# A matrix-memory recurrence and two feed-forward layers on one core: the first expert's weights fetched in 13 pieces of columns

## The chip, the core and the metric

The kernel runs on one core of one Trainium2 chip. The metric is the time of one execution in device microseconds (us), lower is better. The engines are TensorE (PE, its weight loads PEld), VectorE (DVE), ScalarE (ACT), GpSimd (POOL) and the queue of SyncE (SP), which here only issues DMAs. POOL issues the indirect DMAs, those whose rows are picked by an index in memory.

## The reference

The inputs are six arrays of 4 x 8 heads, 768 steps and 40 columns for the recurrence, and the weights of a mixture of 8 experts and of a dense layer. All arithmetic is float32.

```python
state = 0                                        # per head, 40 x 40
for t in range(768):
    y[:, :, t] = einsum('bhd,bhde->bhe', rt, state)
    Sa = einsum('bhde,bhe->bhd', state, at)
    state = state * wt - Sa (x) bt + vt (x) kt   # (x): outer product
x = y as 3072 tokens of 320
logits = x @ w_gate + modality_bias[modality_id]
e_idx = argmax(logits); gate = softmax(logits)[e_idx]
for e in range(8):                               # w1: 320 x 1024, w2: 1024 x 320
    out[mask] = gate * (relu(x[mask] @ w1[e]) @ w2[e])
h = out @ w_in                                   # 320 x 2048
return (h * sigmoid(1.702 * h)) @ w_out          # 2048 x 320
```

## The kernel before, in words

**Three stages.** The recurrence goes in 24 steps of 32 time steps (`NCH`), each turned into matmuls of small blocks; each step ends with a tile Y of 128 tokens x 320 columns. Then come the experts (`moe1`), which take the tokens sorted by expert in tiles of 128 rows, and the dense layer (`moe2`).

**Inside a step c of the recurrence.** `chain(c, g)` works for two groups g of four heads. It makes W from the state (W, X, V, all in PSUM), ends with the tile `ust`, and SP issues a DMA transpose of it, `UE<-ust`. `state` makes the next state (`S`, `s`, `Ss`, and the transpose `Sd<-s`). `output` multiplies `rE` and `UE` in 32 small matmuls (`g<-rE,UE`), masks the result (`mx`, `mgZ`, `zbd`) and multiplies it with `bst` into `y`; DVE makes Y of it. The last step, 23, needs the state of step 22, and its own `UE`.

**Routing.** `row` scales each Y, makes halves of it in `XR` and multiplies them with the gate's weights. Every fourth step, `route` picks the expert of each token of a group, and POOL scatters the rows of `XR` into a sorted table `XD` in memory with one indirect DMA for each step (`XD<-XR,desti`). The groups are steps 0-3, 4-7, 8-11, 12-15, 16-19, 20-22 and 23. One `XR` buffer serves all groups, so that the next group's `XR` waits until the scatters before it have landed. When all is routed, `tables` works out the order of the tiles, and `usual` decides a branch; behind it `moe1` begins.

**The first expert's weights.** After step 19 (`EARLY` is 20) `lead` picks the expert with the most tokens so far. Its number is in `er`, and `w0row` is the row of the weight tables for each partition. Two indirect DMAs bring the weights: `fetch(1)` 128 rows of 3072 numbers into `raw1`, `fetch(2)` 128 rows of 2560 numbers into `raw2`. Two more (`load`, `xg<-XD,xrow`) bring the first two tiles of that expert's rows. ACT and DVE cut the weights into two float16 halves (`split<-raw`), 8 parts of 384 columns and 5 of 512, and PE runs the first two tiles (`first`) between the last steps of the recurrence: the turn of the rows is `v<-id,xg`, the matmuls are `w<-aE,split` and `s<-split,...`.

**What sets the order.** Everything from the recurrence to `first` is recorded and then ordered by a planner (`Plan.emit`): a list scheduler with a cost for each operation, that goes forward and backward nine times (`ROUNDS`) and keeps the order with the shortest planned span. So an instruction's place on its engine follows from the planner's costs, not from the place in the code. For an indirect DMA it counts 1040 ns on POOL, a start of 2450 ns (`DMA_START`) and 0.355 ns for each byte of a partition, during which its one modelled DMA channel takes no other transfer. Between two indirect DMAs in a row POOL gets a `memset` of `between`. All recorded instructions have line 234.

Of the kernel before, what the change touches and what calls it, by code (L numbers as in the profile page):

```python
# [469 lines left out]
I32 = mybir.dt.int32  # L470
U32 = mybir.dt.uint32
AF = mybir.ActivationFunctionType
ALU = mybir.AluOpType
# [15 lines left out]
WS = 256.0  # L489
GROUPS = [(0, 4), (4, 4), (8, 4), (12, 4), (16, 4), (20, 3), (23, 1)]  # L490
EARLY = 20
FIRST = 2


class Mlp:
# [11 lines left out]
    def consts_in(self, p, tp, w_gate, modality, bias):  # L507
        nc = self.nc
# [15 lines left out]
        def iota(shape, pattern, base=0, mult=0):  # L524

            count[0] += 1
            t = tp.tile([128] + shape, I32, name=f"io{count[0]}")
            nc.gpsimd.iota(t, pattern=pattern, base=base, channel_multiplier=mult)
            f = p.tile([128] + shape, F32, name=f"if{count[0]}")
            nc.vector.tensor_copy(f, t)  # L530
            return f
# [6 lines left out]
        nc.vector.tensor_scalar(self.e3072, e4, float(NT), None, op0=ALU.mult)  # L538
        self.q = iota([NTILE], [[128, NTILE]], mult=1)
        self.pf = iota([1], [[0, 1]], mult=1)  # L540
        self.s1 = iota([NSLOT], [[1, NSLOT]], base=1)
        self.s128 = iota([NSLOT], [[128, NSLOT]], mult=1)

# [11 lines left out]
        m = tp.tile([128, NTILE], mybir.dt.int64, name="mod")  # L555
# [117 lines left out]
    def lead(self, ncol, ps):  # L673
# [20 lines left out]
        nc.vector.tensor_scalar(self.w0row, self.er[:, 0, 0:1], 128.0, self.pf, op0=ALU.mult, op1=ALU.add)  # L694
        nc.vector.tensor_scalar(self.xrow[:, 0:FIRST], self.s128[:, 0:FIRST], self.er[:, 1, 0:1], None, op0=ALU.add)

    def small(self, name, shape, dt=F32):
        if name not in self.tabs:
            self.tabs[name] = self.tab.tile([128] + shape, dt, name=name)
        return self.tabs[name]  # L700
# [105 lines left out]
    def weights1(self, wp, W1, W2):  # L806

        self.W1, self.W2 = W1, W2
        parts = []
        for n, w in ((1, NW1), (2, NW2)):  # L810
            raw = wp.tile([128, max(w, 2644)], F32, name=f"raw{n}")
            setattr(self, f"raw{n}", raw[:, 0:w])
            parts.append(raw)
        for n, w in ((1, NW1), (2, NW2)):
            t = wp.tile([128, w], F32, name=f"split{n}")
            h = t.bitcast(F16)
            setattr(self, f"hi{n}", h[:, 0:w])
            setattr(self, f"lo{n}", h[:, w:2 * w])
            parts.append(t)

        xg = wp.tile([128, 1032], F32, name="xg0")
        self.x0 = [xg[:, a:a + XROW] for a in (XROW, 0)]
        self.y0 = [xg[:, a:a + YROW] for a in (2 * XROW, XROW)]
        parts.append(xg)
        left = [[t, 0] for t in parts]

        def lend(n):
            x = next(x for x in left if x[1] + n <= x[0].shape[1])
            x[1] += n
            return x[0][:, x[1] - n:x[1]]  # L830

        return lend

    def fetch(self, n, row):
        self.nc.gpsimd.indirect_dma_start(
# [1003 lines left out]
def body(tc, A, out):  # L1839
    nc = tc.nc  # L1840
    with ExitStack() as ctx:
        m = Mlp(tc, ctx)
        dp = ctx.enter_context(tc.tile_pool(name="dr", bufs=1, space=DRAM))
        XD = m.XD = dp.tile([NE * NT, XROW], I32, name="XD")
        YS = m.YS = dp.tile([NSLOT * 128, YROW], I32, name="YS")
        XF = dp.tile([NT, DM], F32, name="XF")
        m.consts(A["wg"], A["mod"], A["mb"])
        kp = m.tab = ctx.enter_context(tc.tile_pool(name="keep", bufs=1))
        tail = NTILE - 1
        with ExitStack() as c1:  # L1850
            pool = lambda n, b: c1.enter_context(tc.tile_pool(name=n, bufs=b, side="right", reuse_waits="tile"))
            lent = m.weights1(pool("m1w", 1), A["W1"], A["W2"])
            with ExitStack() as c2:
                p = Pool(c2.enter_context(tc.tile_pool(name="rt", bufs=1)), 1)
                ps = Pool(c2.enter_context(tc.tile_pool(name="rps", bufs=1, space=PSUM)), 1)
                at = Attn(tc, c2, A["WU"], A["AB"], A["KVR"], kp, lent)
                plan = m.nc = at.plan
                plan.between = m.between
                Y, sent, read, later = {}, [], [], []

                def sink(c, full=False):
                    if not full:
                        Y[0] = p.tile([128, DM], F32, tag="Y", bufs=2)
                        return Y[0][:, :]
                    plan.after = RTAIL if c == tail else 0.0
                    plan.tail = TAIL if c >= EARLY else 0.0
                    m.row(Y[0][:, :], c, (p, lambda: ps.tile([128, 512], F32, tag="r")))
                    c0 = max(a for a, _ in GROUPS if a <= c)
                    if c == c0 + dict(GROUPS)[c0] - 1:
                        m.route(c0, XD, p, sent if c < EARLY else later)  # L1870
                    plan.tail = WTAIL
                    if c == EARLY - 1:
                        m.lead(EARLY, m.bank[:, 416:424])
                        for n in (1, 2):
                            m.fetch(n, m.w0row)
                        for i, x in enumerate(m.x0):
                            read.append(m.load(i, x))
                            plan.preds[read[-1]].update(sent)
                    plan.tail = TAIL if c == tail - 1 else 0.0

                at.run(sink)
                plan.tail, plan.after = 0.0, RTAIL
                m.tables(m.bank[:, 416:424])
                at.range(kp, m.ones, at.py.bank([8], "y"))
                ok, usual, usualf = m.small("ok", [1], I32), m.small("usual", [1], I32), m.small("usualf", [1])
                at.good(plan, ok, usualf, m)
                plan.vector.tensor_copy(usual, usualf)
                plan.tail, plan.after = LTAIL, 0.0
                for n in (1, 2):
                    m.split(n)  # L1890
                p1, p2 = at.spare()
                m.first(p1, Given(ys=m.y0), p2)
                plan.emit()
                sent, read, later = ([plan.made[i] for i in x] for x in (sent, read, later))
                apart(tc, sent + later)

                for a in read:
                    for b in later:
                        tc.declare_no_dep(a.ins, b.ins, reason="rows of later tiles")
                m.nc = nc  # L1900
            m.before2(ctx)
            m.tab = ctx.enter_context(tc.tile_pool(name="tab", bufs=1, reuse_waits="tile"))
            m.next(pool("m1x", 5))
            for i, x in m.x1.items():
                m.load(i, x)
            rv = nc.values_load(usual[0:1, 0:1], min_val=0, max_val=1)
            with tc.If(rv < 1):
                held = nc.values_load(ok[0:1, 0:1], min_val=0, max_val=1)
                with tc.If(held < 1):
                    slow_attention(tc, A["r"], A["k"], A["v"], A["w"], A["a"], A["b"], XF)  # L1910
                    with tc.tile_pool(name="rt3", bufs=1) as p, tc.tile_pool(name="rps3", bufs=1, space=PSUM) as ps:
                        for c in range(NTILE):
                            X = p.tile([128, DM], F32, tag="Y", name="Y")
                            nc.sync.dma_start(out=X, in_=XF[c * 128:(c + 1) * 128, :])
                            m.row(X, c, (p, lambda: ps.tile([128, 512], F32, tag="r", name="r")))
                            c0 = max(a for a, _ in GROUPS if a <= c)
                            if c == c0 + dict(GROUPS)[c0] - 1:
                                m.route(c0, XD, p)
                        m.lead(NTILE, ps.tile([128, NE], F32, tag="c", name="c"))
                        m.tables(ps.tile([128, NE], F32, tag="c", name="c"))  # L1920
                        for n in (1, 2):
                            m.fetch(n, m.w0row)
                            m.split(n)
                        for i, x in [*enumerate(m.x0), *m.x1.items()]:
                            m.load(i, x)
                        m.first(p, p, ps)
                with tc.tile_pool(name="rt4", bufs=1) as p, tc.tile_pool(name="rps4", bufs=1, space=PSUM) as ps:
                    m.extra(p, ps)
            step = m.weights2(A["wi"], A["wo"], ctx)
            m.moe1(lambda i: step())  # L1930
        m.moe2(out)
# [16 lines left out]
```

## Time and profile before

| | us |
|---|---|
| median of 3 runs | 1115.99 |
| the three runs | 1117.01, 1115.99, 1109.04 |
| the profiled execution | 1107.79 |
| its span, first to last instruction | 1106.0 |

Shares of the span in which the engines are busy: PE 82%, DVE 78%, ACT 61%, POOL 13%. The recurrence lasts to about 550 us, the first two tiles run to about 567 us, the experts to about 760 us, the dense layer to the end. A busy share is an average over stages: what a wait is worth is to be read in its own stage. The profiled execution is one run, taken by itself.

### The profile page before, as it was taken

The page shows a single profiled execution, that of the slowest core. Times are in us where ns is not written, and L with a number is a line of the kernel's source. Part 1 is how long each engine was busy: PE and PEld are TensorE (multiplying, and loading weights), DVE is VectorE, ACT ScalarE, POOL GpSimd, SP SyncE. Part 2 cuts the span into 40 slices and gives each one's busy share as a digit, 9 for nine tenths or more (in the row PEclk, how much of TensorE's full clock was granted, in tenths as well). Part 3 has the DMA queues.
Part 4 walks back from the last instruction along what each step waited for, and adds up shares of the span by engine and source line. Part 5 has one row for each costly group of instructions (what it writes and reads, how often), then busy time and mean ns, then how long its engine had stood idle before and what let it go on. Part 6 is the DMA issues. An engine that isn't in the chain of part 4 may idle for free. (4 is left out here: it accounts for less than half of the span.)

```text
span 1106.0 us, 36977 instructions
## 1 busy us (share of the span) xinstructions
PE 903.8 (82%) x15537; PEld 664.9 (60%) x15537; DVE 858.8 (78%) x2089; ACT 673.9 (61%) x1468; POOL 138.8 (13%) x224
## 2 busy tenths in 40 slices
PE   0167886877778787787768998998999999999995
PEld 0155665666666665675657877885555555555553
DVE  8998998998999889887764788676766666666652
ACT  4477998998899899776722363344343434343432
POOL 2000000020020020011132223213002111111101
PEclk9999897987677678667889998999999999999998
DMA  3669789689979779758527678665011111111100
GB/s 111 128 147 182 142 157 177 115 165 193 177 148 180 127 150 172 132 104 135 157 87 201 151 198 282 149 136 128 7 25 49 30 42 35 39 36 42 38 1 25
DMA packets 250654, 129.91 MB, mean 117 GB/s; under 512 B 234400, under 2 KB 237728, under 8 KB 249312
## 3 DMA queue, kind: packets, MB, share of 16 engines
q1 hardware_dynamic: 244464, 98.09, 48.4%
q0 software_dynamic: 6000, 29.23, 7.7%
q8 instruction: 125, 2.05, 0.8%
q14 instruction: 65, 0.53, 0.2%
HBM read 57.78 MB, written 12.16 MB: 63 GB/s over the span
## 5 line engine op out<-in xcount | busy, mean ns | idle before, releaser
L1160 ACT ACTIVATE sg<-t 128x512 f32<-128x512 f32 x96 | 60.5, 630 | 184.3 <-DVE t L1158 174.3
L1154 PE MATMUL h<-xT,WH 128*128 128x512 f16 x480 | 119.3, 379 | 1.8 <-DVE g L1164 1.8
L1178 PE MATMUL acc<-OH,gh 128*128 128x320 f16 x384 | 114.8, 299 | 1.0 <-ACT gh L1166 1.0
L1178 PE MATMUL acc<-OH,gl 128*128 128x320 f16 x384 | 114.8, 299 | 0.6 <-DVE gl L1170 0.6
L1178 PE MATMUL acc<-OL,gh 128*128 128x320 f16 x384 | 114.8, 299 | 0.0
L1158 DVE TENSOR_TENSOR t<-h,sB 128x512 f32<-128x512 f32 x96 | 66.2, 690 | 52.3 <-PE h L1154 49.0
L870 PE MATMUL h<-xT,split 128*128 128x128 f16 x1536 | 96.8, 226 | 11.4 <-DVEq L916 3.9
L870 PEld LDWEIGHTS <-split 128*128 128x128 f16 x1536 | 93.1, 101 | 15.2 <-DVEq L916 4.8
L1178 PEld LDWEIGHTS <-gh 128*128 128x128 f16 x768 | 74.8, 98 | 44.3 <-ACT gh L1166 1.6
L1170 DVE TENSOR_TENSOR gl<-g,gh 128x512 f16<-128x512 f32 x96 | 66.4, 691 | 43.8 <-ACT gh L1166 39.7
L234 POOL DMA_INDIRECT XD<-XR,desti x24 | 30.9, 1289 | 480.8 <-ACT ust L234 207.0
L884 PE MATMUL y<-split,hh 128*128 128x320 f16 x384 | 83.5, 303 | 5.6 <-DVEq L969 4.7
L1154 PE MATMUL h<-xT,WL 128*128 128x512 f16 x288 | 77.8, 379 | 0.0
L1154 PEld LDWEIGHTS <-WH 128*128 128x128 f16 x480 | 46.6, 98 | 44.8 <-DVE g L1164 3.5
L234 PE MATMUL w<-s,pick 128*128 128x160 f16 x368 | 63.4, 290 | 10.0 <-DVE s L234 2.9
L234 PEld LDWEIGHTS <-kb 64*128 64x128 f16 x2208 | 46.7, 101 | 37.6 <-issue 28.1
L234 PEld LDWEIGHTS <-tbd 128*128 128x128 f16 x1152 | 51.4, 105 | 23.9 <-issue 12.1
L1164 DVE SCALAR_TENSOR_TENSOR g<-h,sg 128x512 f32<-128x512 f32 x96 | 65.4, 681 | 0.0
L1166 ACT CAST gh<-g 128x512 f16<-128x512 f32 x96 | 59.3, 617 | 1.4 <-DVE g L1164 1.4
L884 PE MATMUL y<-split,hl 128*128 128x320 f16 x192 | 58.1, 303 | 0.0
L1186 POOL DMA_INDIRECT out<-o,ti x24 | 23.5, 978 | 273.0 <-ACT o L1184 269.6
L872 ACT ACTIVATE hh<-h 128x512 f16<-128x512 f32 x48 | 28.4, 595 | 46.0 <-PE h L870 39.0
(346 smaller groups left out, 2368.3 us busy)
## 6 DMA issues: line engine op xcount, KB each, us to landing
K<-in_KVR SPq DMA_DIRECT2D x24, 480.0 KB
raw<-in_AB SPq DMA_DIRECT2D x13, 640.0 KB
s<-in_wi SPq DMA_DIRECT2D x12, 512.0 KB
s<-in_wo SPq DMA_DIRECT2D x10, 512.0 KB
raw<-in_WU SPq DMA_DIRECT2D x6, 660.0 KB
YS<-ys SPq DMA_DIRECT2D x24, 160.5 KB
Sd<-s SPq DMA_TRANSPOSE x46
raw<-in_KVR SPq DMA_DIRECT2D x1, 480.0 KB
```

The source lines that it names most:

```text
L234: r = self.made[i] = getattr(getattr(self.nc, e), op)(*a, **k)
L870: nc.tensor.matmul(h[:, f4, :], lhsT=a, rhs=b, start=(j == 0), stop=(j == 7))
L872: nc.scalar.activation(hh[:, s, :], h, AF.Relu)
L884: nc.tensor.matmul(y, lhsT=a[:, f, :], rhs=V(b, f), start=(n == 0), stop=(n == 23))
L1154: nc.tensor.matmul(h3, lhsT=a, rhs=r, start=(j == 0), stop=(j == 7))
L1158: nc.vector.tensor_tensor(t, hs[k], self.xs[steps[k][0]]["sB"], op=ALU.mult)
L1160: nc.scalar.activation(sgs[k], t, AF.Sigmoid, scale=1.702)
L1164: nc.vector.scalar_tensor_tensor(gs[k], hs.pop(k), 2.0 ** -4, sgs.pop(k), op0=ALU.mult, op1=ALU.mult)
L1166: nc.scalar.copy(ghs[k], gs[k])
L1170: nc.vector.tensor_tensor(gls[k], gs.pop(k), ghs[k], op=ALU.subtract)
L1178: nc.tensor.matmul(accs[c], lhsT=a[:, s], rhs=r[:, f, :], start=(f == 0 and j == 0), stop=(f == NF - 1 and j == 2))
L1186: sent.append(nc.gpsimd.indirect_dma_start(out=out, out_offset=bass.IndirectOffsetOnAxis(ap=X["ti"][:, c:c + 1], axis=0), in_=o, in_offset ...
```

## The change

`fetch(1)` and `fetch(2)` of the first expert become 8 and 5 indirect DMAs of 384 and 512 columns (`CUTS`), so that each part that `split` takes has a transfer of its own. The weight tables are seen as k times as many rows of a k-th of the length, and `cuts` works out k row numbers for each partition: two constant tables (`part`) at the kernel's start, and four small DVE instructions after `lead`. In the code the two loads of rows now stand ahead of the pieces. The same bytes are brought; the rest of the code is as before.

```diff
+CUTS = {1: 8, 2: 5}
...
+        self.part = {n: iota([k], [[1, k]], mult=k) for n, k in CUTS.items()}
...
+    def cuts(self):
+
+        nc = self.nc
+        self.cut = {}
+        for n, k in CUTS.items():
+            t, i = self.small(f"cut{n}", [1]), self.small(f"cuti{n}", [k], I32)
+            nc.vector.tensor_scalar(t, self.er[:, 0, 0:1], 128.0 * k, None, op0=ALU.mult)
+            nc.vector.tensor_scalar(i, self.part[n], t, None, op0=ALU.add)
+            self.cut[n] = [i[:, j:j + 1] for j in range(k)]
...
+    def pieces(self, n):
+
+        raw, W, k = getattr(self, f"raw{n}"), getattr(self, f"W{n}"), CUTS[n]
+        for j, i in enumerate(self.cut[n]):
+            w = raw.shape[1] // k
+            self.nc.gpsimd.indirect_dma_start(
+                out=raw[:, j * w:(j + 1) * w], out_offset=None, in_=W.rearrange("r (j x) -> (r j) x", j=k),
+                in_offset=bass.IndirectOffsetOnAxis(ap=i, axis=0))
...
                         m.lead(EARLY, m.bank[:, 416:424])
-                        for n in (1, 2):
-                            m.fetch(n, m.w0row)
                         for i, x in enumerate(m.x0):
                             read.append(m.load(i, x))
                             plan.preds[read[-1]].update(sent)
+                        m.cuts()
+                        for n in (1, 2):
+                            m.pieces(n)
```

Since the planner makes the order, the built programs show what moved. On POOL, behind the last scatter of steps 16-19, there stood before (`raw_150` is `raw1`, `raw_151` is `raw2`, `xg_154` holds the two tiles of rows):

```order
L234 DMA XD<-XR_278,desti 24576x322
L267 MEMSET between 128x1
L234 DMA raw_150<-in_W,w0row 128x3072
L267 MEMSET between 128x1
L234 DMA raw_151<-in_W,w0row 128x2560
L267 MEMSET between 128x1
L234 DMA xg_154<-XD,xrow 128x322
L267 MEMSET between 128x1
L234 DMA xg_154<-XD,xrow 128x322
L234 COPY XR_278<-if_102 128x3
```

There stands now (`raw_159` is `raw2`, `raw_158` is `raw1`; the dots are four more pieces of the one and seven more of the other):

```order
L234 DMA XD<-XR_286,desti 24576x322
L267 MEMSET between 128x1
L234 DMA raw_159<-in_W,cuti_316 128x512
...
L234 DMA raw_158<-in_W,cuti_314 128x384
...
L234 DMA xg_162<-XD,xrow 128x322
L267 MEMSET between 128x1
L234 DMA xg_162<-XD,xrow 128x322
L234 COPY XR_286<-if_110 128x3
```

The planner has put all 13 pieces ahead of the two loads of rows, although the code has them behind, and the five of `raw2` ahead of the eight of `raw1`.

On PE, the first small matmul of step 22 with `UE` stood before behind the product V of the first group (`v`) of step 23:

```order
L234 MATMUL v_263<-X_0_262,nbd 128x40
L234 LDWEIGHTS XR_278
L234 MATMUL r_277<-id_66,XR_278 128x128
L234 LDWEIGHTS UE_270
L234 MATMUL g_238<-rE_257,UE_270 32x32
```

Now the first of them stands ahead of the state's turn (`pick`) of the second group and of the rest `neg` of W of the first:

```order
L234 MATMUL y_242<-Sd_0_282,rE_260 32x40
L234 LDWEIGHTS UE_278
L234 MATMUL g_246<-rE_265,UE_278 32x32
L234 LDWEIGHTS pick
L234 MATMUL w_0_274<-s_218,pick 128x160
...
L234 LDWEIGHTS neg_230
L234 MATMUL w_0_268<-W_0_269,neg_230 128x4x40
```

It has moved forward by 168 rows of PE's program, from row 21897 to row 21729, which is 84 matmuls with their weight loads.

On DVE, behind `er`, there stood before the mask of the step's products, and `w0row` came later:

```order
L234 TENSOR_REDUCE er<-leadr 128x8
L234 SCALAR_TENSOR_TENSOR mx_255<-g_238,mask 128x256
L234 TENSOR_TENSOR S_217<-s_265,P_242 128x320
L234 TENSOR_SCALAR tbd<-TT_248,own 128x16x32
L234 TENSOR_SCALAR er<-er 128x8
```

Now the row numbers of the pieces come at once:

```order
L234 TENSOR_REDUCE er<-leadr 128x8
L234 TENSOR_SCALAR cut_315<-er 128x1
L234 TENSOR_SCALAR cut_313<-er 128x1
L234 TENSOR_SCALAR er<-er 128x8
L234 TENSOR_SCALAR cuti_316<-if_98,cut_315 128x5
L234 TENSOR_SCALAR cuti_314<-if_94,cut_313 128x8
L234 TENSOR_SCALAR ust<-w_0_268 128x4x2x40
```

Beside these places, the order of PE, DVE, ACT and SP differs at many places from about the 13th of the 24 steps on, since the planner's choice among its nine orders starts from other costs. Up to there, and from `moe1` on, the orders of PE, ACT and SP are the same, and DVE and POOL differ only by the constant tables of `part`.

## Rows read from the trace of the kernel before

**Rows 1.** Busy us and (count) of each engine by stretch, granted clock, DMA share, GB/s.

```profile
530.00:536.00 6.00, 6.00 (x161) 5.59 (x158) 4.07 (x14) 5.63 (x15) 0.00 (x0) 0.53 1.06 311
538.00:547.50 9.50, 7.40 (x257) 6.10 (x257) 8.79 (x28) 9.28 (x26) 0.00 (x0) 1.00 0.31 65
547.50:567.50 20.00, 17.34 (x260) 13.63 (x259) 16.05 (x88) 8.49 (x19) 5.09 (x8) 1.00 0.15 48
600.00:640.00 40.00, 40.00 (x514) 34.52 (x512) 29.11 (x48) 13.54 (x23) 8.71 (x12) 1.00 0.67 156
```

**Rows 2.** VectorE's instructions in order of time: start, us, line, operation, tiles.

```profile
523.68 0.20 DVE L234 TENSOR_SCALAR w0row<-er,if 128x1 int32<-128x1 f32 x1
...
555.19 0.48 DVE L234 SCALAR_TENSOR_TENSOR Y<-y,R 128x320 f32<-128x320 f32 x1
...
566.71 0.15 DVE L234 CAST usual<-usualf 128x1 int32<-128x1 f32 x1
```

**Rows 3.** ScalarE's instructions in order of time; in brackets the idle time before.

```profile
535.60 0.52 ACT L234 ACTIVATE split<-raw 128x384 f16<-128x384 f32 x1
...
558.12 0.75 ACT L234 ACTIVATE XR<-Y,sc 128x256 f16<-128x256 f32 x2 [3.48 <-DMA XD<-XR,desti]
```

**Rows 4.** TensorE's matmuls in order of time, at the end of the recurrence.

```profile
531.77 0.71 PE L234 MATMUL w<-s,pick 128*128 128x160 f16 x4
...
537.91 0.22 PE L234 MATMUL v<-X,nbd 128*128 128x54 f16 x2 [1.44 <-issue]
...
538.20 0.38 PE L234 MATMUL g<-rE,UE 120*32 120x32 f16 x32
...
541.45 0.35 PE L234 MATMUL y<-bst,zbd 128*128 128x54 f16 x7 [0.71 <-ACT zbd L234]
...
543.38 0.27 PE L234 MATMUL v<-id,xg 128*128 128x128 f16 x2
...
550.10 0.38 PE L234 MATMUL g<-rE,UE 120*32 120x32 f16 x32 [0.42 <-DMA UE<-ust]
```

**Rows 5.** SyncE's queue in order of time: the transposes of steps 22 and 23.

```profile
524.50 1.26 SPq L234 DMA_TRANSPOSE UE<-ust  x1
...
545.35 1.23 SPq L234 DMA_TRANSPOSE UE<-ust  x1
```

**Rows 6.** GpSimd's instructions in order of time.

```profile
518.89 0.96 POOL L234 DMA_INDIRECT XD<-XR,desti  x1 [0.19 <-issue]
...
524.15 0.98 POOL L234 DMA_INDIRECT raw<-in_W,w0row  x1 [4.18 <-DVE er L234]
...
528.07 1.02 POOL L234 DMA_INDIRECT xg<-XD,xrow  x1 [0.19 <-issue]
...
537.22 0.19 POOL L234 COPY xg<-xg 128x1 f32<-128x1 f32 x1 [7.93 <-DMA xg<-XD,xrow]
...
554.88 1.29 POOL L234 DMA_INDIRECT XD<-XR,desti  x1 [17.48 <-ACT ast L234]
```

**Rows 7.** DMA queues from 525 to 530 us: packets, MB, share of 16 engines.

```profile
q0 software_dynamic: 114, 1.40, 79.4%
q1 hardware_dynamic: 99, 0.03, 2.2%
```

**Rows 8.** DMA queues from 534 to 538 us.

```profile
q1 hardware_dynamic: 1295, 0.32, 76.2%
q0 software_dynamic: 120, 0.54, 37.3%
```

**Rows 9.** Busy us by stretch, as in rows 1, while GpSimd issues indirect DMAs.

```profile
221.00:228.00 7.00, 4.16 (x124) 2.85 (x124) 5.90 (x10) 6.28 (x16) 5.78 (x7) 0.79 1.08 275
480.00:485.00 5.00, 2.42 (x56) 1.60 (x50) 2.18 (x8) 1.77 (x5) 3.08 (x5) 0.84 0.37 135
516.00:521.00 5.00, 0.96 (x12) 0.73 (x12) 0.80 (x5) 0.00 (x0) 3.39 (x8) 0.76 1.24 197
526.00:530.00 4.00, 1.75 (x35) 1.09 (x33) 2.19 (x7) 0.66 (x3) 2.91 (x6) 0.85 0.92 338
```

## The prediction

> **What bounds the kernel now.** I read the table of stretches first, to see which engine sets the end from where on. From 600 us PE is busy all the time (40.00 of 40 us in one stretch, [rows 1]), so whatever the end of the recurrence gains or loses in starting time goes through to the end of the kernel, and nothing else of the change reaches it. The question is thus when the branch behind `usual` (566.71 us, [rows 2]) can be taken, and when PE has done with the first two tiles.
>
> Next, the instructions in order of time, back from there. `usual` hangs on the routing of step 23, and this on its `XR`, which at 558.12 us had waited 3.48 us for a scatter [rows 3], that of step 20, issued at 554.88 us [rows 6]. So two chains end nearly together. One is Y of step 22, its routing, the scatter and the free buffer. The other is Y of step 23 (555.19 us, [rows 2]), which by itself would have let `XR` start sooner than it did. The end comes earlier only if both do, and if PE's own work for the first tiles (17.34 us busy in the 20 us from 547.5, [rows 1]) starts earlier too.
>
> Both chains pass the time of the weight fetch. Three waits there bear on it.
>
> - The transpose of step 22's `UE` was issued at 524.50 us and used at 538.20 us, 13.7 us later. That of step 23, with no fetch beside it, was issued at 545.35 us and used at 550.10 us, after 4.75 us, and there PE waited for it [rows 4, 5]. The queue view says why: from 525 to 530 us the indirect queue q0 held the engines for 79.4% with 114 packets, and the queue of the transposes got 99 packets and 2.2%. When the fetch ebbed, 1295 packets of it went through in 4 us [rows 7, 8].
> - PE stood 1.44 us ahead of `v<-X,nbd` of step 23 at 537.91 us, in that rush of transposes, and 0.71 us for `zbd` at 541.45 us, which is made from step 22's late `UE`; the end of step 23's chain stands behind it on PE [rows 4].
> - From 526 to 530 us PE ran 35 matmuls, where it ran 161 in the 6 us behind it [rows 1, 9].
>
> **The change part by part.** *The two fetches go, 13 pieces come.* On POOL an indirect DMA costs (528.07 - 524.15) / 3 = 1.31 us, its issue, the memset and the gap [rows 6]. Thirteen take 17.0 us where two took 2.6. The row numbers are ready earlier than `w0row` was (523.68 us, [rows 2]), since DVE now makes them right behind `er`, in a stretch where it was busy for 0.80 of 5 us [rows 9]; so pieces can follow the last scatter at 518.89 + 1.31 = 520.2 us. The last one starts at 520.2 + 12 x 1.31 = 535.9 us. An indirect DMA lands 558.12 - 554.88 = 3.2 us after its start by the scatter [rows 3, 6], so the weights are there from 523.4 to 539.1 us. `split` began at 535.60 us [rows 3] and its other parts come after that, one by one between the recurrence's work. The cover holds: cost 0. Without it, each late piece would hold ACT with the recurrence queued behind.
>
> *The loads of rows move behind the pieces*, since the planner put them there. They start at 537.2 and 538.5 us and land at 540.4 and 541.7 us, where before they were seen landed at 537.22 us [rows 6]. PE turns the first tile at 543.38 us [rows 4]. That leaves 543.38 - 540.4 = 3.0 us. The cost is 0, but no more than 3.0 us can be gained before the first tile is late.
>
> *The transposes get room.* A fetched packet was 1.40 MB / 114 = 12.3 KB, a whole row of 3072 numbers, and 79.4% of 16 engines over 5 us, shared by 114 packets, is 0.56 us each [rows 7]. A transpose's packet that takes turns with those waits as long each time. A piece has rows of 1.5 or 2 KB, and comes once in 1.31 us, 128 x 1.5 KB or 2 KB, which is 150 to 200 GB/s. The fetch moved 1.40 MB / 5 us = 280 GB/s at 79.4%, so 353 GB/s is all the engines can give, and pieces hold 43 to 57% of them. If `UE` gets the other half, its 4.75 us become at most twice that in the part that moves data, some 5 to 7 us in all; it lands at 529.3 to 531.5 us. PE now wants it at about 531.8 us, where the turn of the second group's state (`pick`) stood [rows 4]. It fits, barely.
>
> So the 0.71 us go. The 1.44 us go if the rush was what stopped PE; I count both, 2.1 us for step 23's chain, and 538.20 - 531.5 = 6.7 us for step 22's Y, which is then no longer late. The sum is -2.1 us, under the bound of 3.0.
>
> *PE while POOL issues.* The 35 matmuls in 4 us are no single case. In four stretches with bursts of indirect DMAs PE ran 124 in 7 us, 56 in 5, 12 in 5 and 35 in 4 [rows 9], that is 17.7, 11.2, 2.4 and 8.8 a microsecond, against 161 / 6 = 26.8 and 257 / 9.5 = 27.1 without [rows 1]. In the third ACT did nothing and DVE nearly nothing. The trace does not say what stops PE, the issuing or the transfers. The burst grows by 11 DMAs, 14.4 us. If transfers are the cause, the smaller pieces spread it thinner. I take 0, since the bytes are the same; the bounds are -2.7 us (the 4 us at full rate would have had 107 matmuls, so 72 / 26.8 = 2.7 us lost, all back) and a loss that is the rival below.
>
> *Small things.* Two iotas and two casts stand at the kernel's start. Four DVE instructions of about 0.20 us, like `w0row` [rows 2], stand now ahead of step 22's `ust`: 0.8 us at most, in DVE's idle time, so 0. The order of the last 11 steps is another one. The `UE` transposes are 545.35 - 524.50 = 20.85 us apart, one step [rows 5]; half a microsecond each way for a step makes 5.5 us either way over 11 steps. I take 0.
>
> **A rule that speaks against it.** The fetch's packets were 12.3 KB [rows 7]. The Trainium skill, "DMA: Bandwidth & Descriptors", section "SWDGE vs HWDGE vs iDMA", has a packet, the boundary at which an engine turns to another queue, as "≤4096 B preferably". By that a whole row would have come in packets as small as the pieces', the transposes would have waited no longer than they will, and the change would give 0 instead of -2.1 us. The trace does not agree: 1.40 MB in packets of 4 KB would be 342, and it shows 114.
>
> The same page, section "Anatomy of one DMA — SWDGE (gpsimd) path", gives each such DMA a fixed cost of about 2.0 us. Taken one behind the other, 13 would cost 22 us more than two, by estimate. The rows have one start each 1.31 us, so the fixed parts overlap, and I don't add them.
>
> **The rivals.** *Slower: PE is held while POOL issues.* If the issuing itself is what slows PE, it slows it until about 539 us. The work that PE did from 530 to 536 us and in the 2 us behind 538 us, some 161 + 54 = 215 matmuls or 8.0 us, then runs at 17.7 a microsecond (12.1 us, +4.1) or at 11.2 (19.2 us, +11.2). I take +6 us, near the milder end, since step 23's chain is not all of PE's work. For it: four bursts, four slow stretches. Against it: the first was mild, though it had as many DMAs. It decides from the point where less than about 80% of PE's rate is left. A step of the same kind: PE's first matmul with step 22's `UE` now stands ahead of step 23's chain. Landing at 538.20 us as before, it would hold PE for 538.20 - 531.8 = 6.4 us. Both give about +6.
>
> *Nothing: hidden anyway.* The two tiles of rows land later than worked out, or ACT, busy for 9.28 of the 9.5 us from 538 us [rows 1], keeps the start of the first tile where it is. By the skill's packet rule the result is the same. 0 us.
>
> *The new order decides.* A different order of the last 11 steps gives up to 10 us either way, about 0.9 us a step.
>
> **How the numbers follow.** The profiled execution took 1107.79 us, 1.79 more than its span. It is 8.2 below the median of 1115.99; of the four times known, two lie at 1107.8 and 1109.0, two at 1116.0 and 1117.0. I work from their mean, 1112.5: forecast 1112.5 - 2.1 = 1110.4; nothing 1112.5; slower 1118.5, at worst 1112.5 + 11.2 = 1123.7; another order 1102 to 1122. Chances: forecast 0.42, nothing 0.18, slower 0.22, another order 0.18. The range takes in the forecast with its bounds (down to 1112.5 - 3.0, less 4 us for the spread of runs), nearly all of the slower case, and most of the orders: 1102 to 1122. One per cent is 11 us, about what a measurement of this kernel tells from no change. Below that end only a lucky order: 0.16. Above the other, the worst of the slower case and an unlucky order: 0.14. Within: 0.70.
>
> **What would show it.** Right: step 22's `UE` used under 9 us after its issue, packets of q0 under 4 KB, no wait of PE for `zbd` of step 22, the pieces 1.3 us apart from about 520 us, `usual` about 2 us earlier against step 21's `UE` than before. Wrong: PE below 15 matmuls a microsecond up to 540 us (the slower rival), PE waiting on `UE` near 532 us, `v<-id,xg` waiting for the rows, or a difference that is there already at 500 us (the order).

## The result, and the profile after

The changed kernel took 1117.99 us (median of 19 runs, 1114.18 to 1127.86), the kernel before, beside it, 1111.87 us (19 runs). The ratio is 1.0064, interval 1.0041 to 1.0086: 0.64% or 7.1 us slower (the two medians lie 6.1 us apart), where 2.1 us less had been forecast. The ratios here and below leave out executions that ran slow as a whole; the medians do not. The time lies inside the range of 1102 to 1122, the sign is wrong.

The profiled execution took 1120.07 us. At the first of the four scatters of steps 16 to 19 the two traces stand level (515.10 us, 514.99 before), after up to 5.3 us between them on the way (396.2 against 390.9 us at the first scatter of steps 8 to 11); what happens then is read from PE first. Stretches of the changed kernel, PE alone: its busy time and matmuls, granted clock, DMA share, GB/s.

```profile
500.00:514.00 14.00, 10.91 (x340) 0.88 0.95 146
516.00:520.00 4.00, 1.15 (x23) 0.65 1.16 247
520.00:530.00 10.00, 1.97 (x17) 0.50 0.64 182
530.00:540.00 10.00, 1.38 (x10) 0.50 0.42 125
540.00:550.00 10.00, 8.21 (x239) 0.67 0.56 90
```

27 matmuls in 20 us, where PE had run 161 in 6 us before the change [rows 1]. The granted clock sank to its lower level (0.50, 1.2 GHz) while PE did so little. In order of time, PE's matmuls of that stretch stand alone, and ahead of each is idle time that no other engine, DMA or semaphore in the trace explains ("issue"):

```profile
528.25 0.21 PE L234 MATMUL s<-ust,kb 64*128 64x40 f16 x1 [0.53 <-issue]
528.96 0.19 PE L234 MATMUL s<-ust,kb 64*128 64x40 f16 x1 [0.50 <-issue]
531.06 0.19 PE L234 MATMUL s<-ust,kb 64*128 64x40 f16 x1 [1.92 <-issue]
...
539.55 0.25 PE L234 MATMUL s<-ust,kb 64*128 64x40 f16 x4 [0.52 <-issue]
540.74 0.40 PE L234 MATMUL g<-rE,UE 120*32 120x32 f16 x32
```

POOL's instructions in the changed kernel show what lies beside that, and what comes later for it (compare [rows 6]); the last line is the kernel's last scatter:

```profile
520.18 0.99 POOL L234 DMA_INDIRECT raw<-in_W,cuti  x1 [0.19 <-issue]
...
535.26 0.95 POOL L234 DMA_INDIRECT raw<-in_W,cuti  x1 [0.19 <-issue]
544.58 0.94 POOL L234 DMA_INDIRECT xg<-XD,xrow  x1 [8.25 <-PE w L234]
...
571.11 1.56 POOL L234 DMA_INDIRECT XD<-XR,desti  x1 [22.82 <-DVE bE L234]
584.85 0.98 POOL L872 DMA_INDIRECT xg<-XD,xrow  x1 [2.58 <-issue]
1113.98 0.96 POOL L1207 DMA_INDIRECT out<-o,ti  x1 [0.19 <-issue]
```

PE stops with the run of indirect DMAs and comes back 3 us after the last one has been issued. The other engines stand with it: ACT's next instruction of the recurrence, after 16.81 us, and its first `split`:

```profile
539.67 0.30 ACT L234 ACTIVATE V<-v 128x160 f16<-128x160 f32 x1 [16.81 <-remote]
551.35 0.62 ACT L234 ACTIVATE split<-raw 128x512 f16<-128x512 f32 x1
```

Scatter, branch and moe1 follow late: the scatter of step 20 by 571.11 - 554.88 = 16.2 us, the first load of moe1 by 584.85 - 568.43 = 16.4 us.

Yet the span grew by 12.1 us only. The last scatter of the output and the span, of the kernel before and then of the changed one, say why:

```profile
1095.36 0.96 POOL L1186 DMA_INDIRECT out<-o,ti  x1 [0.19 <-issue]
span 1106.0 us, 36977 instructions
```
```profile
span 1118.1 us, 37013 instructions
```

At the last scatter the changed kernel is 18.6 us late. Behind it the kernel before needs 10.6 us to its end, the changed one 4.1 us. So two effects hide in the 7.1 us: some 13.6 us lost ahead of the end, by the traces mostly in the recurrence (16.4 of 18.6 us), and 6.5 us found at an end that the change never touches. That end is one instruction. POOL's closing `DRAIN` (its record is in the trace, not among the lines shown here) lasts 10.14 us in the kernel before and 3.40 us in the changed one; the other engines wait for it, and in the kernel before the last DMA packet had landed at 1097.5 us.

### The profile page after: what moved, and what is told of

The parts are those of the page before. It is cut to its first block, busy times and chain, and to the rows that moved or that the text cites. A ratio compares the mean times of both kernels' runs of the same rounds, so it can differ in the third digit from the quotient of the medians.

```text
span 1118.1 us, 37013 instructions
## 1 busy us (share of the span) xinstructions
PE 903.7 (81%) x15537; PEld 664.1 (59%) x15537; DVE 858.3 (77%) x2092; ACT 675.4 (60%) x1471; POOL 146.0 (13%) x248
## 5 line engine op out<-in xcount | busy, mean ns | idle before, releaser
L1179 DVE TENSOR_TENSOR t<-h,sB 128x512 f32<-128x512 f32 x96 | 66.2, 690 | 52.7 <-PE h L1175 49.5
L234 PE MATMUL w<-s,pick 128*128 128x160 f16 x368 | 62.7, 288 | 11.2 <-ACT Ss L234 4.2
```

The lines of the kernel that those rows point to most:

```text
L234: r = self.made[i] = getattr(getattr(self.nc, e), op)(*a, **k)
L1179: nc.vector.tensor_tensor(t, hs[k], self.xs[steps[k][0]]["sB"], op=ALU.mult)
```

## The experiments

Theory A: issuing indirect DMAs holds PE, whatever they carry. B: their bytes and packets do. C: the planner's new order costs the time, not the pieces. D, formed on the way: `split` stands ahead of late pieces on ACT. E: it belongs to where the program runs. F: the shorter end belongs to the length of POOL's program.

Each set of kernels ran beside the kernel before. "Stretch" is the time, in the profiled execution, from the first scatter of steps 16 to 19 to the first load of moe1; "end" is from the last scatter to the end of the span. The same order of work differs by 2 to 3 us in the stretch from one execution to another (53.4 and 55.8 us in the first and the last row). The profiled executions of whole, thin26 and plain were the longest of theirs (1105.54, 1113.77 and 1113.64 us, where the medians are 1096.18, 1100.16 and 1104.39), that of plain_b the shortest (1086.60 beside 1093.85), so these stretches are not the usual ones.

| run | before, median us | ratio | interval | stretch us | end us |
|---|---|---|---|---|---|
| kernel before | 1111.87 | 1 | | 53.4 | 10.6 |
| the change | 1111.87 | 1.0064 | 1.0041 to 1.0086 | 69.8 | 4.1 |
| whole | 1093.84 | 1.0026 | 0.9992 to 1.0059 | 58.2 | 10.6 |
| thin13 | 1093.84 | 0.9928 | 0.9895 to 0.9961 | 50.0 | 4.0 |
| thin26 | 1093.84 | 1.0072 | 1.0041 to 1.0102 | 65.8 | 4.4 |
| direct13 | 1093.84 | 0.9997 | 0.9960 to 1.0034 | 54.0 | 4.1 |
| before_again | 1096.10 | 1 | | 49.5 | 10.7 |
| after_again | 1096.10 | 0.9933 | 0.9901 to 0.9965 | 52.4 | 4.1 |
| joined | 1096.10 | 0.9986 | 0.9944 to 1.0027 | 52.4 | 10.6 |
| cost1260 | 1096.10 | 0.9978 | 0.9938 to 1.0018 | 59.7 | 4.0 |
| after_third | 1113.53 | 1.0070 | 1.0043 to 1.0096 | 69.8 | 4.1 |
| plain | 1111.82 | 0.9939 | 0.9915 to 0.9963 | 59.8 | 4.1 |
| thin13_b | 1111.82 | 1.0055 | 1.0028 to 1.0083 | 69.0 | 4.0 |
| joined_b | 1111.82 | 0.9995 | 0.9970 to 1.0020 | 54.3 | 10.6 |
| plain_b | 1093.40 | 1.0027 | 0.9998 to 1.0056 | 50.1 | 4.1 |
| plain2 | 1093.40 | 1.0067 | 1.0041 to 1.0093 | 55.7 | 10.6 |
| padded | 1112.86 | 0.9996 | 0.9973 to 1.0019 | 55.8 | 10.6 |

The sets are of two kinds: the kernel before takes 1112 to 1114 us in some and 1093 to 1096 us in others. That was not looked for, and turned out to decide the sign.

**whole.** `CUTS = {1: 1, 2: 1}` in the changed kernel.

> The changed kernel, with each matrix in one piece again: 2 fetches of whole rows, but by the new code and in the new places (row numbers made behind er, loads of rows recorded first, so that POOL has fetch, load, load, fetch). Theory A, issuing holds PE: PE is slow only as long as the 4 DMAs are issued, as before the change; median near the kernel before, 1110 to 1114 us. Theory B, the small packets of the transfer hold PE: packets are 10 to 12 KB again, so the same, 1110 to 1114. Theory C, the planner's new order costs the time, not the pieces: as the changed kernel, 1116 to 1120 us.

Same as the kernel before, so nothing for C; but the set was one of 1094 us, PE ran 147 matmuls in the 5 us from 506 us beside the scatters, and the planner made yet another order of it. The next runs keep the changed kernel's order.

**thin13**, its pieces cut to 8 columns:

```
-   out=raw[:, j * w:(j + 1) * w], in_=W.rearrange("r (j x) -> (r j) x", j=k)
+   out=raw[:, j * w:j * w + 8],   in_=W.rearrange("r (j x) -> (r j) x", x=8)
```

> The changed kernel instruction for instruction on every engine, but each of the 13 pieces brings 8 columns (4 KB in all) instead of 384 or 512, so that nearly no bytes move; the first expert's weights are then those 8 columns over and over, and its output is left wrong. Theory A, issuing: PE is held as in the changed kernel, under 10 matmuls in 2 us from 520 to 536 us, the next row load behind the branch at 583 to 587 us, time 1116 to 1120 us. Theory B, the transfer: PE runs at 20 or more matmuls a microsecond from 520 us on, the row load behind the branch at 564 to 569 us, time 1106 to 1112 us.

Not shown: `split` reads these 8 columns over and over, so that the first expert's output is left wrong, and the planner keeps the price of a full piece. It was 0.7% faster, and PE ran 283 matmuls in the 9 us from 509 us, beside the pieces. Alone that would have been a point for B.

**thin26.** As thin13, and behind each piece in `issue`:

```
+   self.nc.gpsimd.memset(self.between, 0.0)
+   self.nc.gpsimd.indirect_dma_start(*a, **dict(k, out=<the next 8 columns>))
```

> As the run with 8 columns for each piece, but each piece is issued twice (26 DMAs, the second into the 8 columns beside the first), everything else in the same order. Weights as there. Theory A, issuing, at 1.26 us for one: POOL issues until about 552 us, PE is held until then, and the row load behind the branch comes 13 x 1.26 = 16.4 us later than with 13, at 599 to 603 us; time 8 to 16 us over the run with 13. Theory B, the transfer: as with 13, within 1 us. If issuing holds PE only in the group of the scatters and not in that of the pieces, also as with 13.

The times differ by (1.0072 - 0.9928) x 1093.84 = 15.8 us, the number of theory A, and the trace refutes it: PE ran 324 matmuls in the first 10 us while POOL issued, and 156 in the 10 us from 527 us. It stood elsewhere, because the pieces and loads came later. The longest of these waits, on ACT and then on PE:

```profile
525.75 0.52 ACT L236 ACTIVATE split<-raw 128x384 f16<-128x384 f32 x1 [6.95 <-DMA raw<-in_W,cuti]
```
```profile
546.84 0.50 PE L236 MATMUL v<-id,xg 128*128 128x128 f16 x3 [8.38 <-DMA xg<-XD,xrow]
```

**direct13.** The pieces as `gpsimd.dma_start(out=..., in_=W[0:128, columns])`.

> The changed kernel with its 13 pieces as plain DMAs from POOL's queue (a fixed address, expert 0, so the choice of the expert is left out), same bytes, same order on all engines. Theory A1, any DMA that POOL issues holds PE: as the changed kernel, 1116 to 1120 us. Theory A2, only those with row numbers read from SBUF do: PE at 20 or more matmuls a microsecond from 520 us, row load behind the branch at 564 to 570 us, time 1106 to 1113 us. Theory B, the transfer: as the changed kernel, as long as packets are small.

PE ran 314 matmuls from 511 to 521 us, so no hold either, and no gain. Nothing in this set had been held, so the changed kernel itself had to run in another one.

**after_again** and **before_again**, both kernels unchanged.

> The changed kernel once more, on the chip and beside the runs of the other kernels of this set. If what was seen in the profile after (PE at 0 to 2 matmuls in 2 us from 520 to 539 us) belongs to this program, it stands here too and the ratio is 1.004 to 1.009. If it belongs to the chip or the moment, PE runs at 20 or more matmuls a microsecond in the burst as it does in the run with 8 columns, what holds it then is ACT waiting for a piece with the recurrence queued behind, and the ratio may be another one, 0.995 to 1.005.

> The kernel before, for a profile from the same chip: where PE stands in the scatters' burst near 515 us and in the fetch near 525 us. If PE is held by issuing, both show under 10 matmuls a microsecond as in the first profile of before; if that belongs to the chip, both run at 20 or more.

Here the change is 0.67% faster, more than the text had for this case (0.995 to 1.005); without the shorter end it is level. PE is not held. Stretches of after_again, PE alone; pieces were issued from 511.18 to 527.23 us:

```profile
511.00:517.00 6.00, 2.99 (x131) 1.00 1.22 238
517.00:528.00 11.00, 6.93 (x212) 0.69 0.95 255
```

Nor is it held in the kernel before. The four stretches of [rows 9], at the same distances from their bursts, in before_again, PE alone:

```profile
223.50:230.50 7.00, 4.42 (x144) 0.76 0.97 236
476.60:481.60 5.00, 3.77 (x84) 0.76 0.67 188
507.50:512.50 5.00, 3.74 (x103) 0.74 1.30 224
513.60:517.60 4.00, 3.20 (x114) 1.00 0.88 278
```

That is 144, 84, 103 and 114 matmuls, where the same program had run 124, 56, 12 and 35 in the first set.

What PE does wait for in after_again is ACT, which stands for three pieces, theory D:

```profile
522.27 0.52 ACT L234 ACTIVATE split<-raw 128x384 f16<-128x384 f32 x1 [1.20 <-DMA raw<-in_W,cuti]
523.75 0.52 ACT L234 ACTIVATE split<-raw 128x384 f16<-128x384 f32 x1 [0.76 <-DMA raw<-in_W,cuti]
527.21 0.52 ACT L234 ACTIVATE split<-raw 128x384 f16<-128x384 f32 x1 [2.75 <-DMA raw<-in_W,cuti]
```

**joined**: all engines' order as in the changed kernel, but 2 fetches of whole rows at the first pieces' places. `w0row`'s values in `cuti`, and in `emit`:

```
+   if self.whole(i):      # a later piece of a matrix: not issued; the first one brings all of it
+       continue
```

> The changed kernel with every engine's order as it is, but on POOL the first piece of each matrix brings the whole matrix in rows of 10 or 12 KB, and the other eleven pieces are not issued. Same bytes, 2 DMAs instead of 13, rows loaded directly behind. Theory A, the number of issues costs the time: 5 to 16 us faster than the changed kernel, at or under the kernel before. Theory C, the new order costs it: same as the changed kernel within 2 us. Theory D, the splits on ACT stand before their late pieces: the rows are there some 14 us sooner, so ACT waits for them 3 us at most where the 13 pieces hold it longer, and the branch comes 4 to 8 us earlier than with 13.

**cost1260.** `return 1040.0` for an indirect DMA becomes 1260.0.

> The changed kernel, planned anew with 1260 ns instead of 1040 ns for an indirect DMA on POOL, which is what one takes in the profile. Theory D, the planner puts splits ahead of pieces that are late: with the right price the splits move back, ACT waits for pieces under 1 us in all, and the kernel gains 3 to 7 us on the changed one. Theory A: no gain, the 13 pieces still hold PE. Theory C: any change of up to 6 us either way.

In this set the changed kernel is 5.8 us faster than joined, but 6.5 us of that is the end: up to the last scatter the two are alike (1083.29 and 1083.19 us), and ACT waits for pieces in joined too (2.6 and 2.5 us). Theory D stands as a wait; what the wait costs is not shown. The right price did not take it away as expected: ACT still stood 3.1 and 0.9 us for two pieces in cost1260, in yet another order, and the kernel is no faster than the changed one.

**probe**, with **probe_b** and **probe_c**. Not the kernel, and its output is zeros: PE runs a stream of 64-row matmuls, POOL and SP issue bursts beside it, as described in

> Not the kernel: PE runs one unbroken stream of 64-row matmuls and weight loads (24 to a group, each group copied out by ACT), and beside it, one after the other, stand six bursts: 13 indirect pieces of 1.5 and 2 KB rows; 13 indirect ones of 32 bytes; 2 of whole rows; 13 plain DMAs from POOL; 13 plain DMAs from SP; 13 scatters of 1.3 KB rows. The output is zeros. Theory A, issuing holds PE: PE falls under 10 matmuls a microsecond in all bursts from POOL, the 32-byte ones too. Theory B, the packets hold it: in the bursts of pieces, the plain ones and the scatters, not in the 32-byte one. Theory E, it belongs to the chip of the first profiles: on a chip where the kernel before takes about 1095 us PE holds its rate in all six, and on one where it takes about 1112 us it does not.

> The stream of matmuls with six bursts beside it, a third time. Where the kernel before takes about 1112 us: as the two times before, 1 to 5 matmuls a microsecond in the bursts of indirect DMAs. Theory E: where it takes about 1095 us, no burst holds the stream, it runs at 30 or more a microsecond in all of them.

The first fell in a set of 1113.5 us. Stretches of it, PE alone: no burst; 13 pieces; 13 of 32 bytes; 2 whole rows; 13 plain ones of POOL; 13 plain ones of SP; 13 scatters.

```profile
95.00:117.00 22.00, 11.47 (x793) 1.00 0.02 4
78.00:92.00 14.00, 2.37 (x30) 1.00 0.60 174
122.00:136.00 14.00, 2.37 (x28) 1.00 0.04 4
163.00:173.00 10.00, 4.14 (x254) 1.00 0.74 290
196.00:208.00 12.00, 4.39 (x303) 1.00 0.73 242
229.00:237.00 8.00, 3.49 (x248) 1.00 0.80 245
263.00:306.00 43.00, 25.17 (x1451) 1.00 0.15 50
```

Undisturbed, PE runs 36 matmuls a microsecond; beside the runs of 13 indirect DMAs 2, whether they bring 1.5 KB rows or 32 bytes; beside plain DMAs from POOL or SP 25 and 31, at more GB/s. The 13 scatters are indirect too and left PE 34, against what theory A said. They were issued 2.8 to 4.3 us apart, the two runs before them 1.25 us apart; in the kernel before, scatters 1.3 us apart did slow PE to 12 matmuls in 5 us [rows 9]. So theory A stands for indirect DMAs that follow each other closely; a run at several distances was not made. probe_c fell in a set of 1093.4 us; the first three stretches:

```profile
60.00:74.00 14.00, 7.17 (x498) 1.00 0.02 5
78.00:92.00 14.00, 6.97 (x455) 1.00 0.59 174
109.00:123.00 14.00, 6.54 (x436) 1.00 0.06 9
```

No hold, in the same program: 294.55 us where probe took 321.75. probe_b, in a set of 1111.8 us, repeated the first: 34 and 29 matmuls in 14 us, 321.93 us.

**after_third**, the changed kernel beside the first probe.

> The changed kernel once more, beside the probe, on whichever chip this set falls. Theory E: where the kernel before takes about 1112 us here, the ratio is 1.004 to 1.009 and PE stands at 0 to 5 matmuls in 2 us in the pieces' burst; where it takes about 1095 us, the ratio is 0.990 to 0.997 and PE runs through the burst. Theory A or B alone, without the chip: the ratio is over 1 either way.

Theory E's first case, and the profile of the result again: stretch 69.8 us.

**plain**: the address from a register, in `issue`, and no `memset` between two pieces; full computation.

```
+   row = nc.gpsimd.value_load(cuti[0:1, 0:1])      # the expert's first row, once for each matrix
-   nc.gpsimd.indirect_dma_start(out=raw[:, cols], in_=..., in_offset=...)
+   nc.gpsimd.dma_start(out=raw[:, cols], in_=W[ds(row, 128), cols])
```

> The changed kernel with the same 13 pieces in the same places and every other engine's order as it is, but POOL reads the expert's first row into a register (once for each matrix) and issues plain DMAs with that address, in place of indirect ones. Full computation. Theory A2, only indirect DMAs hold PE: PE runs at 15 or more matmuls a microsecond through the burst on either kind of chip, and the ratio is 0.985 to 0.997 on one where the kernel before takes about 1112 us, 0.990 to 1.000 where it takes about 1095. Theory A1 or B (any DMA of POOL, or its packets): 1.004 to 1.010 on the first kind.

> The changed kernel instruction for instruction, each piece bringing only 8 columns, once more. On a chip where the kernel before takes about 1112 us: theory A (issuing indirect DMAs holds PE there, whatever they carry) ratio 1.000 to 1.010 and PE under 5 matmuls a microsecond in the 16 us of the pieces; theory B (their bytes) ratio 0.985 to 0.995 and PE at its rate. On one where it takes about 1095 us: as the first time, 0.990 to 0.996, PE at its rate.

> The changed kernel's order with 2 fetches of whole rows at the first pieces' places, once more. On a chip where the kernel before takes about 1112 us: theory A, 11 issues fewer give back 11 x 1.26 = 13.9 us of held PE at most, some 5 to 14 us, ratio 0.990 to 1.002; if the new order were what costs the time, 1.005 to 1.010. On one where it takes about 1095 us: as the first time, 0.994 to 1.003.

All three fell where PE is held, and all three came out as theory A has it. In thin13_b the pieces ran from 516.47 to 531.50 us (stretches, PE alone):

```profile
517.00:525.00 8.00, 1.62 (x16) 0.50 0.10 12
525.00:534.00 9.00, 0.82 (x6) 0.50 0.04 3
```

22 matmuls in 17 us with hardly a byte moving; in plain, with all bytes and 13 plain DMAs, 262 in 15 us. plain is the fastest full kernel where PE is held (0.9939), but 6.5 of its 6.8 us are the shorter end: without the hold the pieces cost nothing, and bring nothing.

```profile
517.00:532.00 15.00, 9.19 (x262) 0.50 1.06 179
```

**plain_b** and **plain2**. plain again, and plain with one DMA of whole rows for each matrix.

> The 13 pieces as plain DMAs with an address from a register, full computation, once more. Where the kernel before takes about 1112 us: as the first time, 0.991 to 0.997. Where it takes about 1095 us, indirect pieces don't hold PE either, so that plain ones gain nothing over them: 0.990 to 1.000.

> The changed kernel's order with 2 plain DMAs of whole rows, address from a register, at the first pieces' places; full computation. If indirect issues alone cost the time where the kernel before takes about 1112 us, 2 plain ones cost no more than 13 and the ratio is that of the 13 plain pieces or lower, 0.988 to 0.996. If small packets are what lets the transposes through, whole rows hold them up again, and it stands 2 to 6 us over the 13 plain pieces, on either kind of chip.

Where nothing is held, plain DMAs gain nothing: 1.0027, just above the 0.990 to 1.000 expected, and with the end taken off they lose 0.0027 x 1093.4 + 6.5 = 9.5 us, the cause of which was not looked into. plain2 is 0.0040 x 1093.4 = 4.4 us slower than plain_b, but its end is 6.5 us longer, so small pieces show no gain here.

**padded.** The kernel before, and in `emit` 24 memsets of one column on POOL behind the fourth scatter.

> The kernel before with nothing moved, only 24 one-column memsets more on POOL (the number of POOL instructions that the 13 pieces add), issued where POOL idles some 70 us after the first four scatters. In every profile so far the time from the start of POOL's last scatter to the end is 10.6 us in kernels with 1 or 2 fetches and 4.0 to 4.4 us in those with 13 pieces, plain or indirect, on either kind of chip. Theory F, this belongs to the length of POOL's program and not to the fetch: 4.0 to 4.4 us here, everything ahead as in the kernel before, ratio 0.992 to 0.997. Rival, it comes from how the pieces' DMAs are queued: 10.6 us here and ratio 0.998 to 1.002.

Theory F falls: 1.0 within the interval, and the end is as long as ever (1106.3 - 1095.71 = 10.6 us):

```profile
1095.71 0.96 POOL L1190 DMA_INDIRECT out<-o,ti  x1 [0.19 <-issue]
span 1106.3 us, 37001 instructions
```

## Why the prediction was wrong

*The step that failed* is "PE while POOL issues": "I take 0, since the bytes are the same". The trace had shown four bursts and four slow stretches [rows 9], and the text left open whether issuing or transfers slow PE, but priced it by the transfers. Where PE is held it is the issuing (probe, thin13_b). Its size: the changed kernel loses 0.0064 x 1111.87 = 7.1 us and gains 6.5 at the end, so 13.6 us are lost ahead of it. joined_b, the same order with 2 issues, loses nothing (0.9995, and an end as before). 13.6 us for 11 issues is 1.24 us each (1.0 to 1.5 with the 2.8 us either way of joined_b's interval); one takes 1.26 us in the trace.

*The slower rival* had the mechanism, and its end at 539 us was right (539.55). Its price of 6 us met the total by chance: by its own step it was too low, since it took PE's rate as 11 to 18 matmuls a microsecond, and it was 1.4. Its worst, 11.2, was nearer. The reason held against it, that the first burst was mild, has a likely answer: its four scatters were issued from 220.1 to 226.2 us, up to 2.9 us apart, and in the probe scatters so far apart left PE its rate. Where nothing is held PE ran little more in that stretch (144 matmuls against 124).

*Pieces.* 520.18 to 535.26 us, 1.26 us apart: as worked out. The Trainium skill's fixed cost of about 2.0 us for each such DMA ("DMA: Bandwidth & Descriptors", section "Anatomy of one DMA — SWDGE (gpsimd) path") overlaps here again.

*Cover.* Cost 0 was right only because PE was held: the first `split` came at 551.35 us. Where PE runs, ACT waits 4.7 us for three pieces and PE 4.1 us behind it (0.88, 1.22 and 1.97 us): the cover is gone, as the text had named it.

*Loads of rows.* Worked out for 537.2 us, issued at 544.58: POOL waited 8.25 us for a held PE. In after_again they stand right behind the last piece.

*The transposes get room.* The packets of q0 fell from 12.3 to 3.3 KB (1.03 MB in 313 from 525 to 530 us), as said. Where PE is held the transpose of step 22's `UE` came behind the pieces (542.98 us), so nothing could be gained. Where it is not, it was issued at 511.11 us and used from 518.67, 7.6 us later, against 511.44 and 521.35 in before_again; but the stretch is not shorter (52.4 against 49.5 us). The 2.1 us are not seen anywhere.

*The new order* cost nothing that can be measured (joined, joined_b). *The end*, 6.5 us, stood in no step; the text had it that "nothing else of the change reaches" the end of the kernel. In all runs the shorter end goes with 13 or 26 pieces, plain or indirect, 4.0 to 4.4 us, the longer one with one fetch for each matrix, 10.6 us, whatever the set. It is POOL's closing `DRAIN`: 10.1 us in every kernel with 107 DMAs on POOL, 3.4 us with 118, 3.9 us with 131 (thin26). That it is POOL's program length is excluded; why it is shorter behind more DMAs stays open.

So the change by itself, without the end, is worth about +13.6 us where PE is held and (0.9933 - 1) x 1096.1 + 6.5 = -0.8 us, nothing, where it is not.

## What to carry to other kernels

Count what a queue issues, not only what it carries: cutting one indirect DMA into many is free only if nothing else pays for each issue, and here PE did. Where one row number serves all 128 partitions, a register and a plain DMA bring the same bytes; in the kernel PE then ran 262 matmuls beside them in 15 us, where it had run 27 in 20. Compare two traces at marks (scatter, branch, last scatter, end) and not by their totals, and a kernel in more than one set of runs before its sign is believed: here an end 6.5 us shorter hid half of a loss, and made a gain of a kernel that gained nothing.

## What the runs showed of the hardware

Two kinds of surroundings exist for the same program. In one, a run of indirect DMAs that POOL issues 1.25 us apart holds PE's matmuls to about 2 a microsecond. It sets in 1 to 3 us after the first of them (in the kernel before, 514.99 us, PE ran 37 matmuls in the microsecond from 515 and 2 in the next; in probe, 74.95 us, 50 from 77 and 5 from 78), and lasts to 2.5 to 3.3 us after the end of the last (91.12 to 93.61 us in probe, 536.21 to 539.55 in the changed kernel), with no semaphore, DMA or engine named as the cause. In the other the same stream keeps 31 to 33. A lack of instructions does not explain the hold: in probe the instruction queue's packet of 16 KB at 79.37 us took 0.93 us, as before the burst (0.93 to 1.41), and PE ran 30 matmuls in the 14 us from 78 us, where it runs 128 for each such packet. Which of the two a run falls in does not go with the chip alone: the chip of after_again, where PE ran on, was also that of padded, where the kernel before took 1112.86 us. What sets it, and what in the issuing holds PE, no run shows. The kernel before differs by some 17 us between the kinds. Its two profiles, 9.8 us apart at the last scatter, show where they part: they are level to 2.5 us through the first twelve scatters, 3.1 us apart at the sixteenth (482.5 and 479.4 us) and 12.4 us at the first load of moe1 (568.43 and 555.99 us). So the first twelve of its 28 indirect DMAs of the recurrence cost nothing that shows; that the others cost it the rest fits, but was not tried.

The Trainium skill ("SBUF — State Buffer", section "Who interferes with whom") has it that "DMA never contends with a compute engine", and names the port pair that DVE and GpSimd share as the only place of contention. The trace agrees in the main for the transfers (31 matmuls a microsecond beside SP's DMAs at 245 GB/s, 36 with none), but, in the first kind, not for the issue of indirect ones: those of 32 bytes took PE from 36 to 2.

In the undisturbed stream PE ran 128 matmuls and as many weight loads and then paused, once in 3.9 us, with one packet of the instruction queue each time (14 packets in 54 us, 0.23 MB, so 16 KB each). That fits a stream limited by its instructions; no run tried it.
